# Splitting each weight operand into its high and low part in one instruction of 1024 columns instead of two of 512

## The chip, the cores and the metric

The kernel runs on one core of a Trainium2 chip. The metric is the device time of one execution in microseconds (us). Engines are named as the profile names them: PE multiplies matrices, DVE and ACT work on tiles elementwise, POOL is the fourth compute engine, SP issues the transfers. Each works through its own queue of instructions in the order in which the program was written.

## What is computed

```python
def reference(q, k, v, g_norm, moe_*, moe2_*):      # shortened
    kv = einsum('bhsd,bhse->bhde', k, v)            # batch 4, heads 8, seq 576, dim 64
    o = einsum('bhsd,bhde->bhse', q, kv)
    x = o / sqrt(mean(o * o, -1) + 1e-6) * g_norm   # -> 2304 tokens x 512
    p = domain_probs / domain_probs.sum(-1)
    x = sum(p[:, e] * (relu(x @ w1[e]) @ w2[e]) for e in range(4))   # w1 512x1024, w2 1024x512
    logits = x @ phi                                # 32 slots, 4 for each of 8 experts
    slots = softmax(logits, axis=0).T @ x
    y = per expert: relu(slots @ m1[e]) @ m2[e]
    return softmax(logits, axis=1) @ y
```

The change concerns the second step, the sum over four experts with the weights `w1` and `w2`.

## The kernel before, in words

**Products of halves.** Every float32 operand of the experts' products is written as a sum of two float16 parts, high and low, and a product is three float16 matmuls (high by high, high by low, low by high). On top of this the product with `w1` is done by a scheme with 7 products of half-sized blocks instead of 8. Its seven weight operands are B11, B21, B22 (blocks as loaded) and T1 to T4 (differences of blocks). An operand is a page: 128 partitions by 1024 float32 as loaded, or by 2048 float16 as high and low part.

**Preparing weights.** `split` (L598 to L605) makes one part: part 0 is an ACT instruction (L601) that scales and rounds, the high part; part 1 a DVE instruction (L603) that scales the source again and subtracts the high part, the low part. It reads two operands from SBUF, the source and the high part. `PrepW1.put` and `w2_split` call it with `i` = 0 and 1, for one half of the page each, 512 columns. `PrepW1.make` (L635) forms T1 to T4 as differences of pages, 1024 columns, on DVE, for expert 0 mostly on POOL. `w_size`, `w_scale_a`, `w_spread` and `w_scale_b` find a scale per expert before that: largest magnitudes (L532 on DVE for `w1`), a small diagonal `dg` (L548), a PE product `ar` that spreads it over partitions (L554), a few tiny DVE steps.

**The order of the work.** PE's work is a list `main` of steps of about equal length. A step of `mm1` (L887) is one of the 7 products for one half `u` of the columns, 12 matmuls; a chunk of 512 tokens takes 14 steps in the order P1, P2, P6, P5, P7, P3, P4. A step of `mm2` (L950) is 6 matmuls. The tokens stand in five chunks, and the program goes expert by expert through chunks 0 and 1 (`mm1` of chunk 0, `mm2` of chunk 0, then chunk 1), then through the others. After a step of `mm1` ACT copies a result out of PSUM (L912) or DVE adds it to an earlier copy (L917), and then ACT and DVE make the high (L903) and low part (L904) of the hidden values; here these are called evictions. `mm2` reads them, and its own results `y` go out on DVE (L959, L961). `y0` to `y3` are the four token tiles of chunk 0, `y4` to `y7` those of chunk 1.

Everything else is strewn among the steps of `main`. `chain(start, stop, steps)` takes a list of small steps and spreads them evenly over the steps of `main` from start to stop, a step in `mm1` counting 0.55 of one in `mm2`:

```python
            credit += wt[0] * (len(steps) - credit) / max(sum(wt), 1e-3)
            n = min(int(credit + 1e-6), max(1, -(-len(steps) // len(wt))))
...
    chain(m["mm2", 0, 0, 0] + 12 if e == 1 else m["mm1", 0, e - 1, 0], m["end", 0, e - 1, 1] - 1,
          prep_w1(0, e, V) + prep_w2(0, e), 12)
```

For each of experts 1 to 3 one chain holds 4 steps that size `w1`, 5 that scale it, 15 of splits, then 4, 5 and 9 for `w2`: 42. In the chain the high part of one half is issued in the same step as the low part of the half before it. Expert 0's `w1` is split before `main` begins (`w_split`, B11, B21, T1, B22) and in hooks at its steps 1, 5 and 9 (T2, T3, T4); its `w2` by a chain of 18 steps over the first `mm1`. `prep_t2` does the same for differences of `w2` that later chunks use.

Of the kernel before, what the change touches and what calls it, by code (L numbers as in the profile page):

```python
# [46 lines left out]
def attn_moe_softmoe_kernel(ctx: ExitStack, tc: tile.TileContext, qT, k, v, g, dp, w1, w2, phi, m1, m2a, m2b, out):  # L47
# [474 lines left out]
    wpw = {}  # L522
# [84 lines left out]
    class PrepW1:  # L607
# [26 lines left out]
            }[op]()  # L634
            (eng or self.eng).tensor_tensor(out=self.src(op).ap, in0=a.ap, in1=b.ap, op=ALU.subtract)  # L635

        def put(self, op, i, part):
            pgs = wop.setdefault(self.k, {})
            if op not in pgs:
                pgs[op] = Page(True)  # L640
            dst = pgs[op].f16().rearrange("p (s k n) -> p s k n", s=2, k=2)
            split(dst[:, :, i], self.src(op).f32(2)[:, i], wpw[self.k[1], "w1"][1], part)

        def hi(self, op):
            for i in range(2):
                self.put(op, i, 0)

        def lo(self, op):
            for i in range(2):
                self.put(op, i, 1)  # L650

    def prep_w1(g_, e, eng):
        w = PrepW1(g_, e, eng)
        st = []
        if g_ == 0:
            st += [lambda b=b: w_size(e, "w1", b) for b in range(4)]
            st += scale_steps(e, "w1")

        then = {
            B11: lambda: w.make(T2),  # L660
            T2: lambda: w.make(T4),
            T1: lambda: w.t1.release(),
            T4: lambda: (w.drop(0), w.drop(2)),
            T3: lambda: w.drop(1),
            B22: lambda: w.drop(3),
        }
        seq = [(op, i) for op in (B11, B21, T2, T1, T3, B22, T4) for i in range(2)]

        def step(n):
            if n == 0:  # L670
                w.make(T1)
            if n == 2:
                w.make(T3)
            if n > 0:
                op, i = seq[n - 1]
                w.put(op, i, 1)
                if i == 1 and op in then:
                    then[op]()
            if n < len(seq):
                w.put(*seq[n], 0)  # L680
# [3 lines left out]
    def w2_split(e, b, key, i, part):
        pgs = w2p.setdefault((0 if key == b else 1, e), {})
        if key not in pgs:
            pgs[key] = Page(True)
        dst = pgs[key].f16().rearrange("p (s k n) -> p s k n", s=2, k=2)
        src = ("w2", 0 if key == b else 1, e, b)
        split(dst[:, :, i], need(src).f32(2)[:, i], wpw[e, "w2"][1], part)  # L690
        if i == 1 and part == 1:
            drop(src)

    def prep_t2(e, eng):
# [18 lines left out]

        for j in range(2):
            st += [lambda j=j, op=op: make(j, op) for op in (T1, T3, T2, T4)]
            bi = [(b, i) for b in (j, 2 + j) for i in range(2)]
            st += stagger([lambda b=b, i=i: w2_split(e, b, f"t{b}", i, 0) for b, i in bi],
                          [lambda b=b, i=i: w2_split(e, b, f"t{b}", i, 1) for b, i in bi])
            st += [lambda: None, lambda: None] + [lambda b=b: away(b) for b in (j, 2 + j)]
        return st  # L720

    def prep_w2(g_, e):
# [1011 lines left out]
```

## Time and profile before

| | |
|---|---|
| median of 3 runs | 835.88 us (835.71 to 836.25) |
| span of the profiled execution | 834.7 us, 16740 instructions |
| that execution's own time | not given apart from the span; the median of the runs is 1.2 us over the span |
| PE busy | 813.2 us, 97% of the span |
| DVE busy | 524.7 us, 63% |
| ACT busy | 348.8 us, 42% |
| POOL busy | 14.4 us, 2% |
| chain that ended last | PE 87%, DVE 8%, ACT 1%, DMA 1% |

The busy share is an average: the page's 40 slices and the table by stretch show where an engine is full. The chain that ended last says which engine held the program up at each time; the waits say what an idle engine waited for. A group of instructions has a line number, and in the profile the names of buffers stand without their numbers (`pages`, `t`, `y`).

### The profile page before, as it was taken

Reading aid. Unit: us, or ns where it says so; the run is one execution under the profiler, and the core shown is the slowest. Engines: PE = TensorE matmul, PEld = TensorE weight load, DVE = VectorE, ACT = ScalarE, POOL = GpSimd, SP = SyncE. Lnnn points to the kernel's source line nnn. Section 1 sums busy time; section 2 is a strip of 40 time slices with the busy share of each in tenths; the row PEclk is TensorE's granted clock in tenths of the full one; section 3 lists DMA queues with packets and bytes.
Section 4 is the critical chain, followed back from the end, with each engine's and each line's share of the span. In section 5 each row is a group of like instructions: output and inputs, shape, how many; then the busy total and the mean of one; then the engine's idle time right before and its main releaser. Section 6 shows DMA issues by size and latency. Waiting matters only on the chain.

```text
span 834.7 us, 16740 instructions
## 1 busy us (share of the span) xinstructions
PE 813.2 (97%) x7121; PEld 607.7 (73%) x7121; DVE 524.7 (63%) x1028; ACT 348.8 (42%) x686; POOL 14.4 (2%) x16
## 2 busy tenths in 40 slices
PE   7899999999999999999999999999999999999995
PEld 7775848575767676848666678898889888984454
DVE  7889988965995433873754527874588538642303
ACT  3675575552555331734543325241454126421202
POOL 3110000000000000000000000000000000000000
PEclk8899999999999999999999999999999999999998
DMA  8860600295129701034330030054103253669597
GB/s 331 354 253 26 218 35 1 101 356 226 69 84 398 283 1 51 27 127 152 127 101 1 2 102 2 1 178 143 61 2 139 82 186 93 212 235 355 216 379 230
DMA packets 40539, 123.87 MB, mean 148 GB/s; under 512 B 4369, under 2 KB 11409, under 8 KB 40465
## 3 DMA queue, kind: packets, MB, share of 16 engines
q1 hardware_dynamic: 40016, 122.70, 40.2%
q8 instruction: 56, 0.92, 0.5%
q14 instruction: 19, 0.15, 0.1%
q10 hardware_dynamic: 448, 0.10, 0.1%
HBM read 94.47 MB, written 28.31 MB: 147 GB/s over the span
## 4 chain that ended last, share of the span: by engine, by line
PE 87%; DVE 8%; ACT 1%; DMA 1%; issue 1%; DVEq 0%; ACTq 0%
PE p L887 35%; PE y L950 28%; PE m L986 14%; DVE pages L603 2%; PE s L1584 2%; PE so L1614 2%; PE o L332 1%; PE kv L277 1%; DVE t L917 1%; DVE pages L904 1%; PE xT L401 1%; PE x2T L1015 1%; PE lg L1038 1%; DMA dpT<-in_dp 1%; PE f L1648 1%
## 5 line engine op out<-in xcount | busy, mean ns | idle before, releaser
L887 PE MATMUL p<-pages 128*128 128x256 f16 (+1 forms) x3360 | 339.4, 262 | 0.5 <-DVE t L825 0.4
L887 PEld LDWEIGHTS <-pages 128*128 128x128 f16 x3360 | 300.3, 98 | 35.1 <-issue 1.9
L950 PE MATMUL y<-pages 128*128 128x512 f16 x1104 | 246.2, 379 | 1.8 <-DVE pages L904 1.1
L950 PEld LDWEIGHTS <-pages 128*128 128x128 f16 x1104 | 107.5, 98 | 125.6 <-issue 4.1
L986 PE MATMUL m<-pages 128*128 128x256 f16 x1092 | 120.8, 273 | 0.0
L986 PEld LDWEIGHTS <-pages 128*128 128x128 f16 x1092 | 106.7, 98 | 12.4 <-issue 0.2
L601 ACT ACTIVATE pages<-pages,s_w 128x512 f16<-128x512 f32 x112 | 73.5, 711 | 42.4 <-DVE s_w L579 12.2
L603 DVE SCALAR_TENSOR_TENSOR pages<-pages,s_w 128x512 f16<-128x512 f32 x112 | 81.0, 765 | 3.2 <-ACT pages L601 3.2
L917 DVE TENSOR_TENSOR t<-p,t 128x512 f32<-128x512 f32 (+1 forms) x72 | 47.6, 664 | 44.3 <-PE p L887 44.2
L903 ACT ACTIVATE pages<-t 128x512 f16<-128x512 f32 (+1 forms) x72 | 44.0, 611 | 62.9 <-DVE t L917 62.3
L996 DVE SCALAR_TENSOR_TENSOR pages<-m,pc,pages 128x256 f32<-128x256 f32 x91 | 40.8, 480 | 45.9 <-PE m L986 45.7
L912 ACT COPY t<-p 128x512 f32<-128x512 f32 (+1 forms) x72 | 40.0, 567 | 68.3 <-PE p L887 67.9
L904 DVE SCALAR_TENSOR_TENSOR pages<-t,pages 128x512 f16<-128x512 f32 (+1 forms) x72 | 48.4, 672 | 8.4 <-ACT pages L903 7.1
L961 DVE SCALAR_TENSOR_TENSOR pages<-y,pc,pages 128x512 f32<-128x512 f32 x28 | 21.0, 748 | 38.2 <-PE y L950 38.2
L797 ACT CAST pages<-t 128x512 f16<-128x512 f32 (+1 forms) x48 | 25.7, 540 | 43.5 <-DVE t L840 22.8
L959 DVE TENSOR_SCALAR pages<-y,pc 128x512 f32<-128x512 f32 x18 | 13.5, 749 | 28.3 <-PE y L950 28.3
L795 ACT ACTIVATE pages<-pages 128x512 f16<-128x512 f32 (+1 forms) x32 | 17.6, 550 | 26.5 <-DVE pages L829 14.3
L806 DVE TENSOR_TENSOR pages<-t,pages 128x512 f16<-128x512 f32 (+1 forms) x48 | 27.9, 585 | 1.2
L802 DVE SCALAR_TENSOR_TENSOR pages<-pages 128x512 f16<-128x512 f32 (+1 forms) x32 | 18.6, 587 | 10.6 <-ACT pages L795 10.6
L819 ACT COPY t<-p 128x512 f32<-128x512 f32 (+1 forms) x16 | 7.8, 506 | 37.5 <-PE p L887 37.5
L797 ACT CAST pages<-pages 128x512 f16<-128x512 f32 (+1 forms) x16 | 8.5, 538 | 32.9 <-DVE t L844 30.7
L471 ACT CAST pages<-pages 128x512 f16<-128x512 f32 (+1 forms) x36 | 19.2, 561 | 6.1 <-DVE pages L420 5.9
(172 smaller groups left out, 644.0 us busy)
## 6 DMA issues: line engine op xcount, KB each, us to landing
pages<-in_w SPq DMA_DIRECT2D x44, 512.0 KB, 7.2
o<-pages SPq DMA_DIRECT2D x33, 512.0 KB, 9.9
pages<-o SPq DMA_DIRECT2D x33, 512.0 KB, 4.8
pages<-in_m SPq DMA_DIRECT2D x32, 512.0 KB, 6.1
pages<-in_m2a SPq DMA_DIRECT2D x16, 512.0 KB, 4.8
pages<-in_m2b SPq DMA_DIRECT2D x16, 512.0 KB, 10.7
o_t<-pages SPq DMA_DIRECT2D x12, 512.0 KB, 3.0
pages<-o_t SPq DMA_DIRECT2D x12, 512.0 KB, 4.3
```

Of the source, the lines that this page charges most:

```text
L601: nc.scalar.activation(dst[:, 0], src, AF.Copy, scale=s)
L603: nc.vector.scalar_tensor_tensor(out=dst[:, 1], in0=src, scalar=s, in1=dst[:, 0], op0=ALU.mult, op1=ALU.subtract)
L797: nc.scalar.copy(dst, sh(src))
L806: nc.vector.tensor_tensor(out=h[:, 1], in0=sh(src), in1=h[:, 0], op=ALU.subtract)
L887: nc.tensor.matmul(ps[:, fp * n:fp * n + n], l, r, start=(fp + i == 0 and P in first), stop=(fp == 1 and i == len(mms) - 1 and P in end), ...
L903: nc.scalar.activation(hh, src, AF.Relu)
L904: late.append(lambda: nc.vector.scalar_tensor_tensor(out=hl, in0=src, scalar=0.0, in1=hh, op0=ALU.max, op1=ALU.subtract))
L912: nc.scalar.copy(t, ps)
L917: nc.vector.tensor_tensor(out=t, in0=ps, in1=t, op=ALU.add)
L950: nc.tensor.matmul(ps, a, b, start=(u + kk + fp + i == 0), stop=(u == 1 and kk == 1 and fp == 1 and i == 2))
L986: nc.tensor.matmul(ps, l, r, start=(i == 0 and j == 0 and P in (1, 2, 7)), stop=(i == len(mms) - 1 and j == nh - 1 and P in (2, 3, 4)), sk ...
L996: nc.vector.scalar_tensor_tensor(out=x, in0=mbank[b][:, 256 * i:256 * i + 256], scalar=pcs[wk[1]][:, t:t + 1], in1=x, op0=ALU.mult, op1=AL ...
```

## The change

`put` and `w2_split` lose their argument `i`, and `split` gets the whole page: 56 ACT and 56 DVE instructions of 1024 columns stand where 112 and 112 of 512 stood. The lists of steps become shorter with it: the chain of an expert has 31 steps instead of 42 (the 15 steps of `w1` splits become 8, the 9 of `w2` become 5), and is still spread over the same steps of `main`.

```diff
-        def put(self, op, i, part):
+        def put(self, op, part):
...
-            dst = pgs[op].f16().rearrange("p (s k n) -> p s k n", s=2, k=2)
-            split(dst[:, :, i], self.src(op).f32(2)[:, i], wpw[self.k[1], "w1"][1], part)
+            dst = pgs[op].f16().rearrange("p (s m) -> p s m", s=2)
+            split(dst, self.src(op).ap, wpw[self.k[1], "w1"][1], part)
...
-        seq = [(op, i) for op in (B11, B21, T2, T1, T3, B22, T4) for i in range(2)]
+        seq = (B11, B21, T2, T1, T3, B22, T4)
...
-            if n == 2:
+            if n == 1:
                 w.make(T3)
             if n > 0:
-                op, i = seq[n - 1]
-                w.put(op, i, 1)
-                if i == 1 and op in then:
+                op = seq[n - 1]
+                w.lo(op)
+                if op in then:
                     then[op]()
...
-    def w2_split(e, b, key, i, part):
+    def w2_split(e, b, key, part):
...
-            bi = [(b, i) for b in (j, 2 + j) for i in range(2)]
+            bs = (j, 2 + j)
...
-        bi = [(b, i) for b in (0, 2, 1, 3) for i in range(2)]
+        bs = (0, 2, 1, 3)
...
-    chain(0, m["mm2", 0, 0, 0], w2s[:-4], 4)
-    chain(m["mm2", 0, 0, 0] - 2, m["mm2", 0, 0, 0] + 4, w2s[-4:])
+    chain(0, m["mm2", 0, 0, 0], w2s[:-2], 4)
+    chain(m["mm2", 0, 0, 0] - 2, m["mm2", 0, 0, 0] + 4, w2s[-2:])
```

The order of the instructions changes with the number of steps, at three places above all. In the changed kernel lines behind the diff stand 5 lower (L912 for L917, L899 for L904).

First, DVE at the end of the first `mm1` (expert 0, chunk 0). `t5_0_0_0_0` is the temporary of product P5 of chunk 0 and half 0; L917 is an eviction that adds, L904 one that makes a low part, L603 a split. Before:

```order
L603 SCALAR_TENSOR_TENSOR pages_78<-pages_78,s_w1_0_189 128x512 x2
L917 TENSOR_TENSOR t5_0_0_0_1_546<-p1_0_0_0_1_384,t5_0_0_0_1_546 128x512
L904 SCALAR_TENSOR_TENSOR pages_78<-t5_0_0_0_0_531,pages_78 128x2x256
L603 SCALAR_TENSOR_TENSOR pages_78<-pages_78,s_w2_0_555 128x512
L917 TENSOR_TENSOR t6_0_0_0_0_493<-p5_0_0_0_0_518,t6_0_0_0_0_493 128x512
L904 SCALAR_TENSOR_TENSOR pages_78<-t5_0_0_0_1_546,pages_78 128x2x256
L603 SCALAR_TENSOR_TENSOR pages_78<-pages_78,s_w2_0_555 128x512
L917 TENSOR_TENSOR t6_0_0_0_1_516<-p5_0_0_0_1_533,t6_0_0_0_1_516 128x512
L904 SCALAR_TENSOR_TENSOR pages_78<-t6_0_0_0_0_493,pages_78 128x2x256
```

Now:

```order
L603 SCALAR_TENSOR_TENSOR pages_78<-pages_78,s_w1_0_189 128x1024
L912 TENSOR_TENSOR t5_0_0_0_1_534<-p1_0_0_0_1_374,t5_0_0_0_1_534 128x512
L899 SCALAR_TENSOR_TENSOR pages_78<-t5_0_0_0_0_519,pages_78 128x2x256
L603 SCALAR_TENSOR_TENSOR pages_78<-pages_78,s_w2_0_543 128x1024
L912 TENSOR_TENSOR t6_0_0_0_0_483<-p5_0_0_0_0_506,t6_0_0_0_0_483 128x512
L899 SCALAR_TENSOR_TENSOR pages_78<-t5_0_0_0_1_534,pages_78 128x2x256
L603 SCALAR_TENSOR_TENSOR pages_78<-pages_78,s_w2_0_543 128x1024
L912 TENSOR_TENSOR t6_0_0_0_1_504<-p5_0_0_0_1_521,t6_0_0_0_1_504 128x512
L899 SCALAR_TENSOR_TENSOR pages_78<-t6_0_0_0_0_483,pages_78 128x2x256
```

Ahead of the addition into `t6` of half 1 there were four splits of 512; now there are three of 1024, since the two halves of the second `w2` page stood behind it.

Second, DVE at the end of the `mm1` of expert 0, chunk 1, while expert 1's `w1` is prepared. Before, the 12 rows up to the low part of `t6`, half 0 (two more splits stand ahead of them):

```order
L603 SCALAR_TENSOR_TENSOR pages_78<-pages_78,s_w1_1_942 128x512 x3
L917 TENSOR_TENSOR t5_0_0_1_0_1036<-p1_0_0_1_0_901,t5_0_0_1_0_1036 128x512
L603 SCALAR_TENSOR_TENSOR pages_78<-pages_78,s_w1_1_942 128x512
L635 TENSOR_TENSOR pages_78<-pages_78 128x1024
L917 TENSOR_TENSOR t5_0_0_1_1_1055<-p1_0_0_1_1_918,t5_0_0_1_1_1055 128x512
L904 SCALAR_TENSOR_TENSOR pages_78<-t5_0_0_1_0_1036,pages_78 128x2x256
L603 SCALAR_TENSOR_TENSOR pages_78<-pages_78,s_w1_1_942 128x512
L917 TENSOR_TENSOR t6_0_0_1_0_996<-p5_0_0_1_0_1023,t6_0_0_1_0_996 128x512
L904 SCALAR_TENSOR_TENSOR pages_78<-t5_0_0_1_1_1055,pages_78 128x2x256
L603 SCALAR_TENSOR_TENSOR pages_78<-pages_78,s_w1_1_942 128x512
L917 TENSOR_TENSOR t6_0_0_1_1_1017<-p5_0_0_1_1_1042,t6_0_0_1_1_1017 128x512
L904 SCALAR_TENSOR_TENSOR pages_78<-t6_0_0_1_0_996,pages_78 128x2x256
```

Now, from the first split of expert 1's `w1` on:

```order
L603 SCALAR_TENSOR_TENSOR pages_78<-pages_78,s_w1_1_972 128x1024
L635 TENSOR_TENSOR pages_78<-pages_78 128x1024
L912 TENSOR_TENSOR t5_0_0_1_0_1004<-p1_0_0_1_0_879,t5_0_0_1_0_1004 128x512
L912 TENSOR_TENSOR t5_0_0_1_1_1023<-p1_0_0_1_1_896,t5_0_0_1_1_1023 128x512
L899 SCALAR_TENSOR_TENSOR pages_78<-t5_0_0_1_0_1004,pages_78 128x2x256
L603 SCALAR_TENSOR_TENSOR pages_78<-pages_78,s_w1_1_972 128x1024
L912 TENSOR_TENSOR t6_0_0_1_0_960<-p5_0_0_1_0_991,t6_0_0_1_0_960 128x512
L899 SCALAR_TENSOR_TENSOR pages_78<-t5_0_0_1_1_1023,pages_78 128x2x256
L603 SCALAR_TENSOR_TENSOR pages_78<-pages_78,s_w1_1_972 128x1024
L635 TENSOR_TENSOR pages_78<-pages_78 128x1024
L912 TENSOR_TENSOR t6_0_0_1_1_987<-p5_0_0_1_1_1010,t6_0_0_1_1_987 128x512
L899 SCALAR_TENSOR_TENSOR pages_78<-t6_0_0_1_0_960,pages_78 128x2x256
```

Eight splits of 512 stood ahead of that last row, three of 1024 stand there now; the four `make` (L635) and all evictions stand ahead of it in both.

Third, PE at the start of the same `mm1`: `ar_w1_1` is the small product that spreads expert 1's scale. Before, it stood behind both halves of P1, 24 matmuls:

```order
L887 LDWEIGHTS pages_78
L887 MATMUL p1_0_0_1_1_918<-pages_78 128x256
L554 MATMUL ar_w1_1_933<-dg_w1_1_883,ones_85 128x128
L887 LDWEIGHTS pages_78
L887 MATMUL p2_0_0_1_0_945<-pages_78 128x256
```

Now it stands behind the first half of P6, which adds to the same buffer `p1`, 60 matmuls into this `mm1`:

```order
L882 LDWEIGHTS pages_78
L882 MATMUL p1_0_0_1_0_879<-pages_78 128x256
L554 MATMUL ar_w1_1_963<-dg_w1_1_877,ones_85 128x128
L882 LDWEIGHTS pages_78
L882 MATMUL p1_0_0_1_1_896<-pages_78 128x256
```

## Rows read from the trace of the kernel before

**Rows 1.** The page, parts 1 and 2: busy engines, DVE in 40 slices.
```profile
PE 813.2 (97%) x7121; PEld 607.7 (73%) x7121; DVE 524.7 (63%) x1028; ACT 348.8 (42%) x686; POOL 14.4 (2%) x16
...
DVE  7889988965995433873754527874588538642303
```

**Rows 2.** The page, part 5: busy us, mean ns of one, then idle before.
```profile
L601 ACT ACTIVATE pages<-pages,s_w 128x512 f16<-128x512 f32 x112 | 73.5, 711 | 42.4 <-DVE s_w L579 12.2
L603 DVE SCALAR_TENSOR_TENSOR pages<-pages,s_w 128x512 f16<-128x512 f32 x112 | 81.0, 765 | 3.2 <-ACT pages L601 3.2
```

**Rows 3.** Busy time by stretch: PE, PEld, DVE, ACT, POOL, clock, DMA share, GB/s.
```profile
80.00:106.00 26.00, 24.11 (x194) 18.77 (x192) 25.69 (x42) 13.62 (x24) 0.00 (x0) 1.00 0.57 198
106.00:145.00 39.00, 38.77 (x264) 25.95 (x265) 32.30 (x57) 23.50 (x41) 0.00 (x0) 1.00 0.01 4
145.00:283.00 138.00, 138.00 (x896) 87.94 (x894) 103.48 (x173) 68.09 (x116) 0.00 (x0) 1.00 0.57 219
283.00:480.00 197.00, 197.00 (x1637) 138.19 (x1636) 106.26 (x219) 82.32 (x166) 0.95 (x1) 1.00 0.19 69
```

**Rows 4.** Waits of PE from 33 to 145 us: total, times, longest.
```profile
PE y L950 <- DVE pages L904: 1.1, 1, 1.1
PE ar_w L554 <- DVE dg_w L548: 0.9, 1, 0.9
PE y L950 <- DVE pages L603: 0.5, 1, 0.5
PE y L950 <- ACT pages L358: 0.2, 1, 0.2
```

**Rows 5.** Groups of instructions by shape: busy us, mean ns of one, idle.
```profile
L537 ACT ACTIVATE junk<-pages 128x1024 bf16<-128x1024 f32 x16 | 16.9, 1058 | 5.5 <-DMA pages<-in_w 5.4
L707 DVE TENSOR_TENSOR pages<-pages 128x512 f32<-128x512 f32 x24 | 16.4, 685 | 0.1
L635 DVE TENSOR_TENSOR pages<-pages 128x1024 f32<-128x1024 f32 x13 | 15.9, 1219 | 0.2
...
L363 ACT ACTIVATE pages<-pages 128x512 f32<-128x512 f32 x14 | 8.4, 633 | 0.0
```

**Rows 6.** Timeline of the opening, all engines: start us, us, instruction.
```profile
14.17 3.78 ACT L601 ACTIVATE pages<-pages,s_w 128x512 f16<-128x512 f32 x6 [10.71 <-DVE s_w L577]
14.92 6.17 DVE L603 SCALAR_TENSOR_TENSOR pages<-pages,s_w 128x512 f16<-128x512 f32 x6 [0.79 <-ACT pages L601]
16.47 2.75 POOL L635 TENSOR_TENSOR pages<-pages 128x1024 f32<-128x1024 f32 x1 [7.19 <-DMA pages<-in_v]
...
16.91 2.85 DVE L603 SCALAR_TENSOR_TENSOR pages<-pages,s_w 128x512 f16<-128x512 f32 x1
...
21.01 1.21 DVE L635 TENSOR_TENSOR pages<-pages 128x1024 f32<-128x1024 f32 x1
22.15 1.40 DVE L603 SCALAR_TENSOR_TENSOR pages<-pages,s_w 128x512 f16<-128x512 f32 x2
23.48 1.26 DVE L367 TENSOR_REDUCE sacc<-pages 128x8 f32<-128x512 f32 x2
```

**Rows 7.** Timeline at the first change from `mm1` to `mm2`, all engines.
```profile
57.52 0.68 DVE L917 TENSOR_TENSOR t<-p,t 128x512 f32<-128x512 f32 x1
57.93 2.38 PE L950 MATMUL y<-pages 128*128 128x512 f16 x10
...
60.94 0.58 ACT L358 COPY pages<-o 128x512 f32<-128x512 f32 x1
```

**Rows 8.** Timeline of `mm1` of expert 0, chunk 1, PE, and DVE at its end.
```profile
83.23 2.78 PE L887 MATMUL p<-pages 128*128 128x256 f16 x24
...
105.50 1.47 DVE L904 SCALAR_TENSOR_TENSOR pages<-t,pages 128x512 f16<-128x512 f32 x2
...
106.23 10.10 PE L950 MATMUL y<-pages 128*128 128x512 f16 x46 [1.13 <-DVE pages L904]
```

**Rows 9.** The chain that ended last, two dense pieces: start us, us.
```profile
125.62 18.34 PE p L887 x168
...
148.07 16.84 PE y L950 x78
```

More of the change, by code (lines that the diff above doesn't have):

```diff
@@ L640, in put @@
                 pgs[op] = Page(True)
-            dst = pgs[op].f16().rearrange("p (s k n) -> p s k n", s=2, k=2)
-            split(dst[:, :, i], self.src(op).f32(2)[:, i], wpw[self.k[1], "w1"][1], part)
+            dst = pgs[op].f16().rearrange("p (s m) -> p s m", s=2)
+            split(dst, self.src(op).ap, wpw[self.k[1], "w1"][1], part)
         def hi(self, op):
-            for i in range(2):
-                self.put(op, i, 0)
+            self.put(op, 0)
         def lo(self, op):
-            for i in range(2):
-                self.put(op, i, 1)
+            self.put(op, 1)
     def prep_w1(g_, e, eng):
@@ L671, in step @@
                 w.make(T1)
[L672 removed]
+            if n == 1:
                 w.make(T3)
             if n > 0:
[L675 to L677 removed]
+                op = seq[n - 1]
+                w.lo(op)
+                if op in then:
                     then[op]()
             if n < len(seq):
[L680 removed]
+                w.hi(seq[n])
         return st + [lambda n=n: step(n) for n in range(len(seq) + 1)]
[L684 removed]
+    def w2_split(e, b, key, part):
         pgs = w2p.setdefault((0 if key == b else 1, e), {})
@@ L687, in w2_split @@
             pgs[key] = Page(True)
-        dst = pgs[key].f16().rearrange("p (s k n) -> p s k n", s=2, k=2)
+        dst = pgs[key].f16().rearrange("p (s m) -> p s m", s=2)
         src = ("w2", 0 if key == b else 1, e, b)
-        split(dst[:, :, i], need(src).f32(2)[:, i], wpw[e, "w2"][1], part)
-        if i == 1 and part == 1:
+        split(dst, need(src).ap, wpw[e, "w2"][1], part)
+        if part == 1:
             drop(src)
@@ L715, in prep_t2 @@
             st += [lambda j=j, op=op: make(j, op) for op in (T1, T3, T2, T4)]
-            bi = [(b, i) for b in (j, 2 + j) for i in range(2)]
-            st += stagger([lambda b=b, i=i: w2_split(e, b, f"t{b}", i, 0) for b, i in bi],
-                          [lambda b=b, i=i: w2_split(e, b, f"t{b}", i, 1) for b, i in bi])
+            bs = (j, 2 + j)
+            st += stagger([lambda b=b: w2_split(e, b, f"t{b}", 0) for b in bs],
+                          [lambda b=b: w2_split(e, b, f"t{b}", 1) for b in bs])
             st += [lambda: None, lambda: None] + [lambda b=b: away(b) for b in (j, 2 + j)]
@@ L727, in prep_w2 @@
             st += scale_steps(e, "w2")
-        def sp(b, i, part):
-            w2_split(e, b, b, i, part)
-        bi = [(b, i) for b in (0, 2, 1, 3) for i in range(2)]
+        bs = (0, 2, 1, 3)
         return st + stagger(
-            [lambda b=b, i=i: sp(b, i, 0) for b, i in bi], [lambda b=b, i=i: sp(b, i, 1) for b, i in bi]
+            [lambda b=b: w2_split(e, b, b, 0) for b in bs], [lambda b=b: w2_split(e, b, b, 1) for b in bs]
         )
```

## The prediction

> **What bounds the kernel now.** I read the shares first: PE is busy 97% of the span, DVE 63%, ACT 42%, but DVE's slices are full in the first eighth [rows 1]. So an instruction saved on DVE or ACT is worth something only where PE waits for them. The table by stretch shows where that can be: from 145 to 480 us PE is busy 138.00 of 138 and 197.00 of 197 us, from 106 to 145 all but 0.23, from 80 to 106 only 24.11 of 26.0 while DVE works 25.69 of 26.0 [rows 3]. PE's waits between 33 and 145 us are four: 1.1 us for a low part of the hidden values (L904), 0.9 us for the small diagonal of expert 1's scale (L548), and 0.5 and 0.2 us where the first `mm2` begins [rows 4]. Before 33 us PE cannot start, since DVE prepares expert 0 (the timeline of the opening [rows 6]). These three places are all that the change can reach; elsewhere a faster split only makes DVE idle longer.
>
> **What one instruction saves.** Two low parts of 512 columns start at 22.15 and the next DVE instruction at 23.48: 0.665 us each; the pair lasts 1.40, so a single one takes about 0.74 and overlaps its successor by 0.07 [rows 6]. (The mean of 765 ns holds one of 2.85 us [rows 2, 6].) No split of 1024 is in the trace; DVE subtractions go from 685 to 1219 ns with 512 more columns, +0.53 [rows 5], so a whole low part takes 0.74 + 0.53 = 1.27 and occupies DVE 1.20, 0.13 less than two halves. On ACT six high parts take 3.78, the last one 0.71, thus 0.61 apart [rows 6]; from 633 to 1058 ns is +0.43 for 512 columns [rows 5], so a whole one takes 1.14, occupies 1.04, and saves 0.18. Over 56 pairs that is 7.3 us of DVE and 10 us of ACT. Bounds for the whole low part: 1.20 if only columns count once more, 1.33 if nothing is saved; I take 1.20, because the subtraction reads two operands from SBUF as the split does.
>
> [...]
>
> **The opening, 14 to 33 us: 0.** It gains columns of overhead and loses a stagger. The first low part can start only when a whole high part is there: 14.17 + 1.14 + 0.04 = 15.35 instead of 14.92. The second starts at 16.55. POOL's difference T2 overwrites the page that the first low part reads; it was issued at 16.47, 0.14 after the second half ended, and the DVE instruction that started at 16.91 then took 2.85 us: while POOL ran, DVE stood [rows 6]. It ended 0.54 after POOL (16.47 + 2.75 = 19.22; 16.91 + 2.85 = 19.76). Now POOL asks at about 16.75 and gets through when the second low part ends, 17.8, instead of at about 16.95, and ends at 17.8 + 2.3 = 20.1. The third low part then needs 0.54 + 0.53 and ends at 21.2, T3 starts at 21.1 (before 21.01), B22's low part at 22.25 (22.15), and the reduction that PE's start hangs on at 23.45 (23.48). What the later start costs, the fewer instructions behind POOL give back. T2 itself, 0.9 us late, is needed only after 36 us. Bounds -0.1 and +0.3.
>
> [...]
>
> **The first `mm2`, 58 to 62 us: +0.1.** Ahead of the addition into `t6` of half 1 stand three whole splits (3.60) for four halves (2.66), so it moves from 57.52 to about 58.5 [rows 7]. PE begins `mm2` at 57.93 as before [rows 7]. Its 0.5 us wait was for the second `w2` page, which is now ready by 58.7; it waits instead for the low part of `t6`, half 0, right behind that addition: 58.5 + 0.6 + 0.7 = 59.8, eight matmuls after 57.93. Then the 0.2 us wait: ACT's copy L358 frees a bank and started at 60.94 [rows 7]; now three ACT evictions follow 58.5 + 0.7, at most 0.63 each (the 633 ns form [rows 5]), so it starts near 61.05. Behind this DVE and ACT still have work that PE reaches later. Bounds -0.2 and +0.5.
>
> **Expert 0, chunk 1, 80 to 106 us: -1.4.** Here DVE is the bound, and the shorter list of steps counts more than the shorter instructions. PE resumed at 106.23, when the low part of `t6`, half 0, ended; it is the first of the two that start at 105.50 [rows 8]. Up to it the old order has eight halves of splits, the new one three whole ones; evictions, the four differences L635, sizing and tiny steps are the same. That is 8 x 0.665 - 3 x 1.20 = 1.72 us less DVE work in a stretch in which DVE idled 0.31 us [rows 3]. I take off 0.3 for the first low part, which waits for a whole high part (between 0, if ACT is ahead, and the 0.43 by which that is longer). So the low part ends near 104.8. PE gets there at 83.23 + 18.34 for 168 matmuls + 0.3 for the small product = 101.9, plus eight of `mm2` at 16.84/78 = 0.216: 103.6 [rows 8, 9]. It still waits 1.2 us, so DVE sets the time and the 1.4 reach PE whole. The 0.9 us wait for the diagonal vanishes: its product moves from 24 matmuls into this `mm1` to 60, that is to 83.23 + 60 x 0.109 = 89.8, and even behind the eviction of `y3` and the low parts of chunk 1 the diagonal is there near 88.5. But it lay inside DVE's 1.72 and adds nothing.
>
> **Where it costs or gives nothing.** Four whole splits of that `w1` move into the `mm2` behind (six halves stood there); DVE is busy 32.30 of 39.0 there [rows 3], and a `y` has two banks, so its eviction may be 2.6 us late (two steps of six matmuls). From 145 to 480 DVE has 103.48 of 138 and 106.26 of 197 [rows 3]: splits stay hidden, and only a DVE that falls behind would show (a rival below). On SP loads and stores of weights move a few places; the DMA share of 0.01 from 106 to 145 [rows 3] shows expert 2's weights already there, some 20 us early, which is the cover. POOL keeps its instructions.
>
> **Sum.** 0 + 0.1 - 1.4 = -1.3 us, against a profiled span of 834.7, which lies 1.2 under the median of 835.88: a span of 833.4, a time of **834.6 us**. A measurement of this kernel can tell about 0.2%, 1.67 us: faster is below 834.21, slower above 837.55. By the bounds of the three places this case reaches from 833.9 to 835.4.
>
> **Rivals.**
> - *The waits eat it.* Every low part now waits for a whole high part, 0.43 longer; three of them in the full stretch make 1.3 and cancel the 1.4: 835.9 us. For it: DVE had 0.31 us of slack there. Against it: ACT is busy 13.62 of 26.0 [rows 3] and issues the high part a step ahead.
> - *More than that.* Evictions come earlier by ACT's 0.18 per pair as well, and the 1.2 us wait left at 104.8 and the 0.7 at the first `mm2` go too: 834.6 - 1.9 = 832.7 us. Against it: both hang on DVE's queue, which has no gap.
> - *Slower: evictions behind long splits.* At each of the eight changes from `mm1` to `mm2` (four experts, chunks 0 and 1) PE's ninth matmul needs the low part of `t6`, and a split ahead of it is 0.54 longer. The result of P3, half 0, comes 36 x 0.109 + 8 x 0.216 = 5.6 us before that need [rows 9]; three evictions, the low part and a split take 4 x 0.61 + 1.20 = 3.6. It decides where DVE is over 2.0 us behind. At all eight: 834.6 + 4.3 = 838.9 us; at the four of experts 0 and 1: 836.7. Against it: PE had no wait after 145 us.
> - [...] If DVE starts its third low part and T3 before POOL gets in, POOL runs from 20.1 to 22.4 and holds up B22's low part instead, and the reduction comes at 23.7: +0.2, 834.8 us. For it only that nothing shows who wins between two longer instructions; the one instance went to POOL.
>
> That the change does less than it says is excluded: the program has 56 and 56 instructions.
>
> **Numbers.** My forecast 0.50, the waits 0.20, more 0.13, slower 0.10, the port 0.07. Faster by over 0.2%: the case of "more", 0.13, and the part of my case in which almost none of the 1.72 is lost, 0.18: 0.31. Slower: nearly all of the slow case, and a little for what I have not seen: 0.11. Within 0.2%: 0.58. The range runs from "more" to the slow case at half its boundaries, 832.7 to 836.7.
>
> **What would show it.** Right: whole splits of 1.27 and 1.14 us, 1.20 and 1.04 apart; POOL's T2 ending near 20.1 and the reduction at 23.4 to 23.5; no wait of PE for the diagonal of expert 1; PE resuming `mm2` of chunk 1 near 104.9, still behind L899; no PE wait from 145 to 480. Wrong: a low part that occupies DVE over 1.3; PE waits for low parts at the later changes; a resumption at 106 or before 104.

## The result and the profile after

The changed kernel takes 842.64 us (median of 840.67, 841.03, 844.26 and 845.40), the kernel before on the same chip 835.8: a ratio of 1.008, 95% interval 1.006 to 1.0099. The prediction was 834.6 us in a range of 832.7 to 836.7: wrong, in sign and in size. The profiled execution is the one of 840.67 us, one of the two faster ones; its span is 838.9 us against 834.7 before. A few executions of these programs, of the kernel before too, had a mean granted clock of 0.85 or less and took at least 13% longer; they stand in no ratio here.

The page's busy engines and DVE's 40 slices, which answer to [rows 1], and the two groups of splits, which answer to [rows 2]:

```profile
PE 814.6 (97%) x7121; PEld 608.0 (72%) x7121; DVE 520.5 (62%) x972; ACT 338.3 (40%) x630; POOL 13.9 (2%) x16
...
DVE  6889978874886443772755426875488538742403
...
L601 ACT ACTIVATE pages<-pages,s_w 128x1024 f16<-128x1024 f32 x56 | 61.4, 1142 | 66.0 <-DVE s_w L577 26.5
L603 DVE SCALAR_TENSOR_TENSOR pages<-pages,s_w 128x1024 f16<-128x1024 f32 x56 | 72.1, 1317 | 7.2 <-ACT pages L601 7.0
```

The instructions save what was worked out: a whole high part takes 1.14 us, a whole low part 1.27 (the mean of 1.317 holds one of 3.38 that POOL held up). DVE is busy 4 us less, ACT 10 us less, and the time is longer. So PE must have got something to wait for. Its waits from 33 to 480 us, to be compared with [rows 4] (lines behind the diff stand 5 lower):

```profile
PE p L882 <- DVE t L912: 4.1, 2, 2.0
PE y L945 <- DVE pages L899: 1.6, 2, 1.5
PE y L945 <- ACT pages L358: 0.5, 1, 0.5
PE p L882 <- DVE pages L603: 0.3, 1, 0.3
```

The first row is new. The table by stretch says where it is; its rows answer to [rows 3]:

```profile
80.00:106.00 26.00, 25.31 (x202) 19.51 (x199) 25.32 (x39) 12.11 (x18) 0.00 (x0) 1.00 0.51 177
...
145.00:283.00 138.00, 133.92 (x874) 85.67 (x873) 97.95 (x143) 62.77 (x88) 0.00 (x0) 1.00 0.54 207
283.00:480.00 197.00, 197.00 (x1599) 136.68 (x1598) 106.39 (x210) 79.49 (x157) 0.95 (x1) 1.00 0.22 78
```

From 145 to 283 us PE was busy all the time [rows 3]; now it stands 4.08 us, in a stretch where DVE is busy only 97.95 of 138. The start times of PE's pieces in the two timelines (us) show where each microsecond of the profiled span went:

| PE starts | before | after | difference |
|---|---|---|---|
| first `mm1` | 33.09 | 32.87 | -0.22 |
| first `mm2` | 57.93 | 59.62 | +1.69 |
| `mm1` of expert 0, chunk 1 | 83.23 | 84.85 | +1.62 |
| `mm2` after it, resumed | 106.23 | 106.76 | +0.53 |
| `mm1` of expert 1, chunk 1 | 164.74 | 165.26 | +0.52 |
| `mm2` after it | 183.08 | 185.81 | +2.73 |
| `mm1` of expert 2, chunk 1 | 243.30 | 246.03 | +2.73 |
| `mm2` after it | 261.64 | 266.57 | +4.93 |
| last product of the program | 825.05 | 830.01 | +4.96 |

Three things happen: the opening loses 1.7 us (1.9 of it behind the first `mm1`), expert 0's chunk 1 gives 1.1 back, and two stalls cost 2.2 each. (The end of the span moves only by 4.2, since what comes behind the last product is 0.8 shorter. Why the median lies another 2.0 us above the time of the profiled execution comes up with the experiment that has halves in the opening alone.)

**The stalls.** The timeline of DVE and PE around the first of them, changed kernel:

```profile
146.34 2.47 DVE L603 SCALAR_TENSOR_TENSOR pages<-pages,s_w 128x1024 f16<-128x1024 f32 x2
152.09 0.38 PE L554 MATMUL ar_w<-dg_w,ones 128*128 128x128 f32 x2
152.29 0.75 DVE L956 SCALAR_TENSOR_TENSOR pages<-y,pc,pages 128x512 f32<-128x512 f32 x1 [3.48 <-PE y L945]
...
172.21 2.47 DVE L603 SCALAR_TENSOR_TENSOR pages<-pages,s_w 128x1024 f16<-128x1024 f32 x2
174.59 1.28 DVE L912 TENSOR_TENSOR t<-p,t 128x512 f32<-128x512 f32 x2
175.33 10.64 PE L882 MATMUL p<-pages 128*128 128x256 f16 x96 [2.04 <-DVE t L912]
```

And the same places in the kernel before:

```profile
147.69 0.38 PE L554 MATMUL ar_w<-dg_w,ones 128*128 128x128 f32 x2
148.11 0.29 DVE L557 TENSOR_REDUCE ar_w<-ar_w 128x1 f32<-128x128 f32 x1 [0.76 <-PE ar_w L554]
151.99 0.75 DVE L961 SCALAR_TENSOR_TENSOR pages<-y,pc,pages 128x512 f32<-128x512 f32 x1 [0.98 <-PE y L950]
...
171.42 1.28 DVE L917 TENSOR_TENSOR t<-p,t 128x512 f32<-128x512 f32 x2
```

Read it from the end. P5 takes the PSUM bank that P2 leaves: both draw from a pool with two buffers, one for each half. (A bank here is one of these buffers, 128 x 512 float32 in the program.) So PE can begin P5, 72 matmuls into the `mm1`, only when DVE's addition L912 has read P2. That addition began 6.68 us after the `mm1` before (171.42 - 164.74), and 9.33 us after it now (174.59 - 165.26). PE is there after 72 x 0.109 = 7.9 us [rows 9]; before, the addition of the first half, one of the two, was done after 6.68 + 0.64 = 7.3, so there was a slack of 0.5 us, and now it is done 2 us too late. DVE came late mainly because it idled: 3.48 us ahead of the eviction of `y0`, and 0.46 later on, against 0.76 and 0.98 before. It idled because nothing that it could do stood ahead in its queue: the next expert's splits need its scale, and the scale needs the product `ar`, which stands 4.4 us later on PE (152.09 for 147.69). With the chain at 31 steps in place of 42 over the same steps of `main`, the ninth step, the last of the scale, stands 9/31 = 29% of the way along instead of 9/42 = 21%. By this reading, which the experiments test, the small steps at the head of the chain went back, behind `y0` whose eviction waits for PE, and the same heap of differences and splits came after them, up against the next `mm1`. The chain of expert 3 does the same one expert later (the second stall, 2.04 us as well).

**The opening.** DVE and POOL some 6 us after the first `mm1` began, kernel before:

```profile
38.91 0.42 DVE L422 TENSOR_TENSOR pages<-pages 128x256 f32<-128x256 f32 x1
39.13 3.44 POOL L635 TENSOR_TENSOR pages<-pages 128x1024 f32<-128x1024 f32 x1 [19.91 <-issue]
39.25 0.42 DVE L423 TENSOR_TENSOR pages<-pages 128x256 f32<-128x256 f32 x1
...
41.63 1.48 DVE L904 SCALAR_TENSOR_TENSOR pages<-t,pages 128x512 f16<-128x512 f32 x1
```

Changed kernel:

```profile
39.58 0.42 DVE L422 TENSOR_TENSOR pages<-pages 128x256 f32<-128x256 f32 x1
39.74 2.48 POOL L635 TENSOR_TENSOR pages<-pages 128x1024 f32<-128x1024 f32 x1 [19.84 <-DVE pages L603]
39.92 2.58 DVE L423 TENSOR_TENSOR pages<-pages 128x256 f32<-128x256 f32 x1
...
49.94 3.88 PE L882 MATMUL p<-pages 128*128 128x256 f16 x34 [0.28 <-DVE pages L603]
```

POOL's L635 makes T4. Before, DVE's short subtractions ran on, POOL took 3.44 us, and only a low part behind them was held up, 1.48 us instead of 0.68; now POOL gets in at once, and a subtraction of 0.42 us takes 2.58. What follows on DVE is late by it, T3's low part among it, for which PE waits at 49.94. The subtraction's record ends 0.28 us after POOL's (42.50 and 42.22); what makes the one stand while the other runs is not shown. Nor can it be read from the start of a record which goes first: before, POOL's record began at 39.13, ahead of DVE's L423 at 39.25, and DVE went first all the same, in its 0.42 us. Over all profiles with T4 on POOL, those of the experiments below included, the four with whole splits in the opening show the long subtraction and nine of the ten with halves the short one; what decides it is not shown. The granted clock was low for longer too, at 0.50 from 31 to 37 us, and from 31 to 34 in the kernel before: the first 48 matmuls took 7.50 us, and 6.04 in the kernel before. Which of the two sets the loss, the experiments had to tell.

Two more rows answer to [rows 6] and [rows 8], POOL's T2 in the opening and the `mm2` that resumes:

```profile
16.63 3.27 POOL L635 TENSOR_TENSOR pages<-pages 128x1024 f32<-128x1024 f32 x1 [7.43 <-DVE pages L603]
...
106.76 12.69 PE L945 MATMUL y<-pages 128*128 128x512 f16 x58 [1.45 <-DVE pages L899]
```

### The profile page after: what moved, and what is told of

Its sections match the earlier page's. It is cut to its first block, busy times and chain, and to the rows that moved or that the text cites. A ratio compares the mean times of both kernels' runs of the same rounds, so it can differ in the third digit from the quotient of the medians.

```text
span 838.9 us, 16624 instructions
## 1 busy us (share of the span) xinstructions
PE 814.6 (97%) x7121; PEld 608.0 (72%) x7121; DVE 520.5 (62%) x972; ACT 338.3 (40%) x630; POOL 13.9 (2%) x16
## 4 chain that ended last, share of the span: by engine, by line
PE 66%; DVE 3%; issue 1%; ACT 1%; DVEq 0%; ACTq 0%
PE p L882 26%; PE y L945 16%; PE m L981 14%; PE s L1579 2%; PE so L1609 2%; PE o L332 1%; PE x2T L1010 1%; PE lg L1033 1%; PE kv L277 1%; DVE pages L603 1%; PE f L1643 1%; PE sp L1104 1%; DVE pages L899 1%; PE xT L401 1%; DVE t L912 0%
## 5 line engine op out<-in xcount | busy, mean ns | idle before, releaser
L601 ACT ACTIVATE pages<-pages,s_w 128x1024 f16<-128x1024 f32 x56 | 61.4, 1142 | 66.0 <-DVE s_w L577 26.5
L603 DVE SCALAR_TENSOR_TENSOR pages<-pages,s_w 128x1024 f16<-128x1024 f32 x56 | 72.1, 1317 | 7.2 <-ACT pages L601 7.0
L912 DVE TENSOR_TENSOR t<-p,t 128x512 f32<-128x512 f32 (+1 forms) x72 | 47.5, 666 | 44.7 <-PE p L882 43.9
L899 DVE SCALAR_TENSOR_TENSOR pages<-t,pages 128x512 f16<-128x512 f32 (+1 forms) x72 | 47.5, 663 | 2.4 <-ACT pages L898 0.6
L473 DVE TENSOR_TENSOR pages<-pages 128x512 f16<-128x512 f32 (+1 forms) x34 | 20.4, 631 | 2.2 <-ACT pages L471 2.2
L792 ACT CAST pages<-pages 128x512 f16<-128x512 f32 (+1 forms) x16 | 8.6, 540 | 32.6 <-DVE t L839 32.5
```

The lines of the kernel that those rows point to most:

```text
L601: nc.scalar.activation(dst[:, 0], src, AF.Copy, scale=s)
L603: nc.vector.scalar_tensor_tensor(out=dst[:, 1], in0=src, scalar=s, in1=dst[:, 0], op0=ALU.mult, op1=ALU.subtract)
L792: nc.scalar.copy(dst, sh(src))
L899: late.append(lambda: nc.vector.scalar_tensor_tensor(out=hl, in0=src, scalar=0.0, in1=hh, op0=ALU.max, op1=ALU.subtract))
L912: nc.vector.tensor_tensor(out=t, in0=ps, in1=t, op=ALU.add)
```

## The experiments

Each ran beside the kernel before, whose median on those chips was 836.28 to 836.53 us; ratios are to it, with the 95% interval behind them. Two theories for the stalls: *pacing* (the number of steps moved the chain's work) and *length* (a whole split in DVE's queue is itself what PE waits for).

**Whole splits, old pacing.** Empty steps stand where the second halves stood:

```diff
-        return st + [los[-1]]
+        st.append(los[-1])
+        return [f for g in st for f in (g, lambda: None)][:-1]
...
-        return st + [lambda n=n: step(n) for n in range(len(seq) + 1)]
+        return st + [(lambda n=n: step(n // 2)) if n % 2 == 0 else (lambda: None) for n in range(2 * len(seq) + 1)]
...
```

> Whole splits of 1024 as in the change, but empty steps fill the lists, so that the chains have their old 42 and 18 steps again. Pacing theory (the shorter list puts the scale steps later, DVE idles, and a heap of splits then stands ahead of the evictions that PE needs): PE's two waits of 2.04 us for the addition L912 at 173 and 254 us are gone, no wait over 0.3 us from 145 to 480; time 836 to 837.5. Length theory (an eviction waits behind one long split): the two waits stay at 1.5 us or more each; time 839 to 841.

837.09 us, ratio 1.0008 (0.9999 to 1.0016). The row of the stretch of the stalls:

```profile
145.00:283.00 138.00, 138.00 (x896) 87.98 (x895) 101.30 (x145) 63.85 (x88) 0.00 (x0) 1.00 0.56 215
```

PE is dense again, with every split whole. The 0.8 us that are left are no more than what the opening costs (below).

**Half splits, new pacing.** The change, with `split` issuing two instructions of 512 in each step:

```diff
+        for c in (slice(0, 512), slice(512, 1024)):
             if part == 0:
-            nc.scalar.activation(dst[:, 0], src, AF.Copy, scale=s)
+                nc.scalar.activation(dst[:, 0, c], src[:, c], AF.Copy, scale=s)
...
```

> The change's steps (31 and 12 in place of 42 and 14), but each split again as two instructions of 512, issued in the same step. Pacing theory: both waits of PE for L912 are there, 2 to 3 us each since the heap of splits is a little larger; time 838 to 840. Length theory: no such wait; time 835 to 836. Opening: the first 48 matmuls of expert 0 take 6.0 us as before the change (7.5 with it), if the whole splits there are what moved the clock.

843.3 us, ratio 1.009 (1.0075 to 1.0104). PE's new wait:

```profile
PE p L883 <- DVE t L913: 5.2, 2, 2.6
```

With the lengths of before the stalls are there, and longer, as was expected of halves, which are more work. The time lies above the 838 to 840 expected. The two runs settle it for pacing.

**Whole splits in the opening alone.** The kernel before, with whole pages in expert 0's `w_split`:

```diff
-            w.hi(op)
-            w.lo(op)
+            for part in range(2):
...
+                split(pgs[op].f16().rearrange("p (s m) -> p s m", s=2), w.src(op).ap, wpw[0, "w1"][1], part)
```

> The kernel before with whole splits for expert 0's w1 alone (before the main list and in its hooks), everything else in halves and with 42 steps. Opening theory (the later first low part shifts PE's work so that the higher clock comes back later): first 48 matmuls 7 to 7.5 us, time 836.5 to 837.5, runs spread by over 1 us. If the opening is neutral: 835.5 to 836 and runs within 0.8 us. No wait of PE for L917 or L912 after 145 us by either.

837.26 us, ratio 1.0012 (1.0003 to 1.002). PE's first `mm2` begins at 59.60, as in the change (59.62).

**Whole splits everywhere but there.** The change, in which `split` issues halves while the opening's `w_split` calls it:

```diff
...
+        if fine[0]:
+            for c in (slice(0, 512), slice(512, 1024)):
...
         def w_split(op):
+            fine[0] = True
             w.hi(op)
             w.lo(op)
+            fine[0] = False
```

> The change, but expert 0's w1 split in halves of 512. Opening theory: first 48 matmuls 6.0 us, 1.2 to 1.5 us less than with the change, runs within 1 us: 838 to 840. The two waits of 2.04 us stay by the pacing theory and by the length theory. If the opening is neutral: as the change, 840.5 to 845.

839.74 us, ratio 1.0047 (1.0033 to 1.0061); the two stalls of 2.04 us are there. So the opening costs about 1.0 us by itself (0.3 to 1.7 by the interval of the run before), and the change without it is still some 3.5 us slower. This run's times lie in two groups, 839.26 to 839.99, and 842.03 and 842.54, and its profile, of the execution of 842.03 us, shows what the upper one has. PE after the first stall, and the table by stretch there:

```profile
173.80 12.31 PE L893 MATMUL p<-pages 128*128 128x256 f16 x96 [2.04 <-DVE t L923]
...
174.00:175.00 1.00, 1.00 (x11) 0.89 (x10) 0.90 (x2) 1.00 (x3) 0.00 (x0) 1.00 0.86 209
175.00:176.00 1.00, 1.00 (x8) 0.74 (x6) 0.74 (x2) 1.00 (x3) 0.00 (x0) 0.56 0.97 397
176.00:177.00 1.00, 1.00 (x6) 0.70 (x5) 0.00 (x0) 1.00 (x4) 0.00 (x0) 0.50 1.02 418
```

Behind the stall the granted clock falls to 0.50, and 96 matmuls take 12.31 us instead of the 10.64 of the changed kernel's profile, where it did not fall. It fell behind both stalls of this execution (12.31 us behind the second too), which makes 3.3 us. The profile of the half splits with the new pacing shows both prices in one execution, behind its first stall and behind its second:

```profile
174.81 12.17 PE L883 MATMUL p<-pages 128*128 128x256 f16 x96 [2.60 <-DVE t L913]
257.90 10.64 PE L883 MATMUL p<-pages 128*128 128x256 f16 x96 [2.59 <-DVE t L913]
```

The changed kernel's four times lie in two groups as well, some 4 us apart: 840.67 and 841.03 us with a mean granted clock of 0.986 and 0.988, and 844.26 and 845.40 with 0.984 and 0.983. None of the upper group was profiled; that its two executions lost the clock behind the stalls is inferred.

**The scale early, the rest dense**, against **the scale late, nothing else changed.** In the first, 11 empty steps stand at the end of the chains of experts 2 and 3 (with halves in the opening); in the second, 4 empty steps ahead of the scale in the kernel before:

```diff
-              prep_w1(0, e, V) + prep_w2(0, e), 12)
+              prep_w1(0, e, V) + prep_w2(0, e) + [lambda: None] * (11 if e > 1 else 0), 12)
```

```diff
-            st += scale_steps(e, "w1")
+            st += [lambda: None] * (4 if e > 1 else 0) + scale_steps(e, "w1")
```

> The change with the opening's halves, and 11 empty steps put at the end of the chains of experts 2 and 3, so that their scale steps come as early as in before and only the splits of w1 behind them stay dense. Delayed scale (y0's eviction and the product ar stand behind scale steps that come too late, DVE idles 3.5 us and then has a heap to work off): no wait of PE for the transposes' eviction after 145 us, PE dense there, 834.8 to 836.2 us. Dense splits (too much split work for each stretch of matmuls): both waits of about 2.0 us stay, 839 to 840.5 us as the change with the opening's halves.

836.51 us, ratio 1.0002 (0.9993 to 1.0011). P2's addition comes at 169.37 behind the start of an `mm1` that began at 164.61, 4.8 us, and no wait for it is left. The stretch is not dense, though: four times PE waits about 0.2 us for an eviction of `y` (L967), and the time misses the 834.8 to 836.2 expected.

```profile
PE y L956 <- DVE pages L967: 0.8, 4, 0.2
...
147.24 0.29 DVE L557 TENSOR_REDUCE ar_w<-ar_w 128x1 f32<-128x128 f32 x1 [0.40 <-PE ar_w L554]
...
169.37 1.44 DVE L923 TENSOR_TENSOR t<-p,t 128x512 f32<-128x512 f32 x2
```

> The kernel before (halves, 42 steps), with 4 empty steps ahead of the scale steps in the chains of experts 2 and 3, so that these come about as late as in the change; nothing else differs. Delayed scale: DVE idles some 3 us ahead of the eviction of y in mm2 of expert 1 and again of expert 2, and PE then waits 1 to 2 us twice for the transposes' eviction, 838 to 842 us. Dense splits: nothing is denser than before, no such wait, 835.7 to 836.5 us.

838.27 us, ratio 1.002 (1.0011 to 1.0029):

```profile
151.94 0.75 DVE L961 SCALAR_TENSOR_TENSOR pages<-y,pc,pages 128x512 f32<-128x512 f32 x1 [3.89 <-PE y L950]
...
172.86 1.28 DVE L917 TENSOR_TENSOR t<-p,t 128x512 f32<-128x512 f32 x2
173.59 10.64 PE L887 MATMUL p<-pages 128*128 128x256 f16 x96 [0.66 <-DVE t L917]
```

Putting the scale back alone, in a kernel that had no stall, makes both: DVE idles 3.89 us ahead of `y0`, and PE waits 0.66 twice, less than the 1 to 2 us expected. That is a third of the 2.04: P2's addition starts 7.95 us after its `mm1` (172.86 - 164.91), between the 6.68 of before and the 9.33 of the change. The full stall appeared only where the late scale and the shorter chain came together; an early scale is enough to remove it.

**The instructions alone, and the best pacing.** Whole splits from expert 0's second chunk on, halves in the opening; first with all chains paced as before, then with expert 1's chain in 31 steps and only the others paced as before:

```diff
...
+        if e == 1:
+            return st + [lambda n=n: step(n) for n in range(len(seq) + 1)]
+        return st + [(lambda n=n: step(n // 2)) if n % 2 == 0 else (lambda: None) for n in range(2 * len(seq) + 1)]
```

> Whole splits from expert 0's second chunk on, halves in the opening, all chains paced as before in 42 and 18 steps: the saving of the instructions alone. Pacing theory: no wait of PE after 145 us, the whole splits are about 4 us less work on DVE and 10 on ACT, none of it on PE's path, 835.6 to 836.3 us, the same as before within 0.1%. Length theory: waits after 145 us, over 837 us.

(The first is the edit with empty steps from above.) 835.95 us, ratio 0.9992 (0.9983 to 1.0001): the saved work, 6 us of DVE and 9 of ACT in this run, is worth nothing that can be told.

> Whole splits from expert 0's second chunk on, the opening as before (halves), the chain of expert 1 in 31 steps, the chains of experts 2 and 3 paced as before in 42 and 18. Pacing theory (the loss came from where the steps of experts 2 and 3's chains stand, the opening's from its clock): PE never waits for the transposes' eviction after 145 us, mm2 resumes from chunk 0 to chunk 1 of expert 0 in 21.9 instead of 23.0 us, first 48 matmuls near 6.0 to 6.6 us, and the time is 834.5 to 835.6 us, 0.7 to 1.5 us under before. Length theory (a whole split in DVE's queue is itself what PE waits for): waits of 1 to 2 us stay after 145 us, 838 us or more.

835.67 us, ratio 0.9988 (0.9979 to 0.9996): 0.8 us faster, a little over the 834.5 to 835.6 expected. From the `mm1` of expert 0, chunk 1, to the resumed `mm2` PE takes 105.75 - 83.85 = 21.90 us, as in the change (21.91), for 23.00 before, and the stretch of the stalls is dense. With whole splits and the old pacing it takes 22.68, with halves and 31 steps 22.06: most of this gain is pacing. In the whole time the two runs of this pair lie only 0.28 us apart, with intervals that overlap, so there the gain is not told apart. The one place where a shorter chain helped is kept, and the two where it hurt are not.

**The opening: clock or POOL?** 20 small products that nothing reads fill PE's 2.9 us of idleness ahead of the second pair of transposes:

```diff
         norms(0)
+        keep(20, ps_x("keep2"), ident, ident)
         squares(1)
```

> The version with whole splits from expert 0's second chunk on and expert 1's chain alone in 31 steps, and in the opening 20 small products on the identity in PE's idle 2.9 us ahead of the second pair of transposes; nothing reads them. If PE's idleness is what brings the granted clock to 0.5 there, the clock stays at 1.0 from 28 to 36 us, the 8 transposes take 1.1 instead of 1.8 us and the first 48 matmuls 5.4 instead of 6.6, and up to 1.8 us come off: 833.8 to 835.2 us. If the clock falls all the same, or DVE's splits ahead of the first mm2 take the gain, 835.0 to 836.0 us as without them.

834.69 us, ratio 0.9981 (0.9972 to 0.9991).

> The kernel before (halves, 42 steps) with the same 20 small products in PE's idle 2.9 us. Clock theory: the first 48 matmuls take 5.4 instead of 6.0 us, 834.6 to 835.8 us. Otherwise the time of before, 835.8 to 836.6 us.

835.33 us, ratio 0.9989 (0.998 to 0.9998). The granted clock is 1.0 throughout from 28 to 39 us in both, and the first 48 matmuls take 5.40 us. Without filling, how long the clock stayed low differed between executions, also with the same halves in the opening: the first 48 matmuls took 6.04 us in the kernel before and 7.27 with the instructions alone. So the 7.50 of the change need not be the whole splits' doing. The 20 float32 products are 40 instructions and take 4.63 us, so the transposes came at 32.67 instead of 31.33; half of them would have done (below). The profile of the first of the two runs, its slowest execution (835.78 us), is also the one with halves in which POOL got in at T4:

```profile
39.44 2.58 DVE L423 TENSOR_TENSOR pages<-pages 128x256 f32<-128x256 f32 x1
```

> The kernel before with whole splits in expert 0's w1 alone, and the 20 small products. Clock theory of the opening's loss (the whole splits cost about 1 us there since the clock stays at 0.5 twice as long): with the clock held the loss is gone up to the 0.28 us wait for a split, 834.6 to 836.0 us, within 0.4 us of the kernel before with the same products. If the loss is in the splits themselves, it stays about 1 us slower than that kernel, 835.8 to 837.2 us.

837.12 us, ratio 1.0009 (1.0 to 1.0018): with the clock held the loss against the same kernel with halves is not gone, it is 1.8 us. The clock theory of the opening falls. Its profile shows what else there is:

```profile
39.28 2.47 POOL L635 TENSOR_TENSOR pages<-pages 128x1024 f32<-128x1024 f32 x1 [19.31 <-DVE pages L603]
39.45 2.58 DVE L423 TENSOR_TENSOR pages<-pages 128x256 f32<-128x256 f32 x1
...
49.46 3.89 PE L887 MATMUL p<-pages 128*128 128x256 f16 x34 [0.93 <-DVE pages L603]
```

A slow PE had only hidden that T3's low part is late: the wait is 0.93 here, 0.28 in the change, where PE came later. So T4 was made on DVE, with the 20 small products, once with halves and once with whole splits in the opening. *Port theory* is the author's name for the view that POOL's T4 gets in between DVE's short subtractions and holds one of them up, as the 2.58 beside 2.47 above shows it; that the two engines share a port no run shows.

```diff
-                lambda: (x_split(1), w_split(T2), w.make(T4), [a_comb(p, nc.vector, (1,)) for p in pp]),
+                lambda: (x_split(1), w_split(T2), w.make(T4, nc.vector), [a_comb(p, nc.vector, (1,)) for p in pp]),
```

> The kernel before with the 20 small products, and expert 0's T4 made on DVE in place of POOL (one DVE instruction of about 1.2 us in place of POOL's of 2.3 to 3.4). Control for the next kernel: 834.8 to 836.2 us by either theory.

835.74 us, ratio 0.9989 (0.998 to 0.9997).

> Whole splits in expert 0's w1 alone, the 20 small products, T4 made on DVE. Port theory of the opening (the whole split ends so that POOL's T4 gets in between DVE's short instructions and holds one of them up 2.2 us, so that T3's low part is late): no DVE instruction of 256 columns lasts over 1 us there, PE's wait for T3's low part (0.9 us with POOL) is under 0.4, and the time is within 0.5 us of the kernel with halves and T4 on DVE. Splits themselves: the wait of 0.9 us and the 1.8 us between whole and halves stay.

836.38 us, ratio 0.9994 (0.9985 to 1.0002). PE's wait for T3's low part, and that low part:

```profile
47.27 1.28 DVE L603 SCALAR_TENSOR_TENSOR pages<-pages,s_w 128x1024 f16<-128x1024 f32 x1 [0.28 <-ACT pages L601]
...
48.62 3.88 PE L887 MATMUL p<-pages 128*128 128x256 f16 x34 [0.43 <-DVE pages L603]
```

No subtraction of 256 columns takes over 0.42 us any more. Without POOL there the difference between whole and halves falls from 1.8 to 0.6 us (in the profiles, at the resumed `mm2`, from 1.48 to 0.47): about two thirds went with POOL's T4, as far as medians with intervals of 0.8 us either way tell. The port theory had expected a little more, a wait under 0.4 and at most 0.5 us of difference. Most of the rest goes with the stagger: a whole low part waits for a whole high part and starts 47.27 - 46.85 = 0.42 us later than the first half did.

**The best version.** The kernel with the best pacing and 10 small products, with halves in the opening, and with whole splits there and T4 on DVE:

```diff
-        keep(20, ps_x("keep2"), ident, ident)
+        keep(10, ps_x("keep2"), ident, ident)
```

> The version with whole splits from expert 0's second chunk on, expert 1's chain alone in 31 steps, and 10 small products (20 instructions of 0.12 us) in place of 20 (which took 4.63 us and made the transposes 1.2 us late): the transposes start at 31.4 instead of 32.6, clock still 1.0, and the time is 833.4 to 834.6 us; 834.7 if DVE's splits ahead of the first mm2 set the time there anyway.

833.95 us, ratio 0.9967 (0.9955 to 0.9979): faster than both kernels, by 2.5 us against the one before. Here POOL did not get in ahead of L423, so the step from 20 to 10 products is not the only difference between the two profiles.

```profile
28.15 2.40 PE L257 MATMUL keep<-ident 128*128 128x128 f32 x20
31.32 1.16 PE L401 MATMUL xT<-ident,pages 128*128 128x128 f32 x8 [0.77 <-DVE pages L390]
```

> All splits whole, the opening's too, T4 on DVE, expert 1's chain alone in 31 steps, 10 small products. Port theory: the whole splits cost the opening nothing once POOL is out of the way, 833.2 to 834.8 us, as with halves there. Splits themselves: 1 us or more over the version with halves in the opening, 834.8 to 836 us.

834.97 us, ratio 0.9983 (0.9975 to 0.9992), 1.0 us over the one with halves. By its own expectation this goes to the splits themselves and against POOL as the only cause, which fits the third that was left above. Only 0.42 of it stands at the resumed `mm2` (104.93 against 104.51), 0.78 at the last product; where the rest arose was not followed up. Halves in the opening remain the better choice.

## Why the prediction was wrong

- **What one instruction saves: right.** 1.27 and 1.14 us for the whole parts, as worked out, and 10 us less on ACT. DVE is busy 4.2 us less where 7.3 were expected; 1.4 of the rest is POOL's, which holds up L423 by 2.2 and no longer the low part that it held up by 0.8 before. What is left, 1.7, was not followed up.
- **The opening up to the first `mm1`: right.** POOL's T2 ended at 19.90 (20.1 expected), the reduction started at 23.24 (23.45), PE 0.22 us earlier; but 0.14 of that stood already at the first high part (14.03 for 14.17), ahead of all that the change touches.
- **The opening behind it: missed, +1.9 for 0** (from -0.22 to +1.69). The sum stopped at 33 us and took T2 as the only work of POOL that splits could meet. T4 is made on POOL too, in the hook at step 1, right behind T2's split. The rival in which DVE goes first and POOL's difference holds up a later low part had the right two engines at the wrong place, and the wrong winner: POOL got in and DVE stood. Its 0.07 stands in the numbers as "the port"; a port no run shows, the runs show a subtraction of 0.42 us that takes 2.58 beside POOL's 2.48, and a POOL subtraction of 3.44 where DVE went first. In this profile 1.46 of the 1.9 stand at the first 48 matmuls, at the low clock; with the clock held, POOL's T4 and the stagger alone cost 1.48 at the resumed `mm2`. The two hide each other and do not add up.
- **The first `mm2`: +0.1 expected, -0.07 measured** (25.30 us from its start to the next `mm1` before, 25.23 after), inside its bounds.
- **Expert 0, chunk 1: right in kind, -1.09 for -1.4.** The wait for the diagonal vanished, PE waits 1.45 us for L899 instead of the 1.2 foreseen, and so 0.3 of the gain is missing. The prediction had put the shorter list ahead of the shorter instructions, and the halves at 31 steps bear it out: 0.9 of the 1.1 is there without any longer split.
- **"Where it costs or gives nothing": this step failed, by 4.4 us.** It argued from DVE's share, 103.48 of 138 [rows 3], that splits after 145 us stay hidden. A share does not say when the work can be done. The prediction looked at expert 1's chain, whose shorter list brought a gain, and did not place the same nine steps in the chains of experts 2 and 3, which run over other steps of `main`. There the scale came behind `y0`, DVE idled first and was late afterwards, and the slack at P2's addition was only 0.5 us. That slack could have been read from the trace before. The 2.0 us by which the median lies above the profiled execution fit a clock that fell behind these same stalls in two of the four executions; that is inferred.
- **The slow rival** had long splits ahead of evictions at the changes from `mm1` to `mm2`. The stalls are in the middle of `mm1`, at the addition that frees P5's bank, and length is not their cause. So its 0.10 was given to a mechanism that did not happen; the true one was not on the list, and that the time came out on the slow side is no credit to it.

## What to carry over

Where small work is spread evenly over a list of steps, the number of small steps is a parameter of the schedule: merging two of them moves everything else in the list, and each chain must be followed to its tightest deadline, here a PSUM bank with 0.5 us to spare. Merge the instructions and keep the pacing, then try pacing as a change of its own. An engine that is 71% busy, as DVE is here from 145 to 283 us (97.95 of 138), can still be late if it idles ahead of a dependency and finds its work in a heap behind it.

## What the runs showed of the hardware

- After a stall of 2.04 us PE's granted clock fell to 0.50 in one profile and stayed at 1.00 in another of nearly the same program; the fall cost 1.67 us over 96 matmuls. With stalls of 2.60 and 2.59 us one execution shows both, 12.17 and 10.64 us. In these profiles the same wait has two prices.
- Behind 2.9 us of idleness in the opening the clock fell in all profiles without filling (to 0.50 from 31 to 34 us in the kernel before), and the first 48 matmuls took 6.04 to 7.50 us; with 40 instructions of 0.12 us in the gap it stayed at 1.00 and they took 5.40, and the kernel before gained 1.2 us by it. Its times also lie closer then: 834.99 to 835.75 us over 11 executions, against 835.46 to 837.60 over 26 of the kernel without filling on the same chip.
- A DVE subtraction of two SBUF operands, 0.42 us, took 2.58 beside a POOL subtraction of 2.48. In the kernel before the POOL subtraction took 3.44 instead and the next low part on DVE 1.48 instead of 0.68. With halves in the opening the first happened in one profile and the second in nine.
- One low clock hid another loss: with PE slower, the wait for T3's low part was 0.28 us, with PE at full clock 0.93. Removing one bound showed the next.
